# Eight small row sums split five and three around ScalarE's copies, in a fused RWKV-6 and mixture-of-depths kernel

## The chip, the core and the metric

The kernel runs on one core of a Trainium2 chip. The engines used are TensorE (PE in the profile, its weight loads PEld), VectorE (DVE), ScalarE (ACT), GpSimd (POOL) and SyncE (SP), which here only issues DMAs. Each engine works through its own instructions in the order in which the program gives them; semaphores make it wait for others. The metric is the device time of one execution in microseconds. Before the change, four runs took 201.69, 201.75, 202.72 and 203.75 us; their median is 202.24 us.

## What is computed

The first stage is an RWKV-6 recurrence over 768 steps for 4 batches and 8 heads of 48 channels. The second is a mixture of depths: each batch's 128 best rows of 768 get a small two-layer network.

```python
for t in range(S):                                   # per batch and head
    cur = (u * k[t])[:, None] * v[t][None, :]
    y[t] = r[t] @ (state + cur)
    state = w[t][:, None] * state + k[t][:, None] * v[t][None, :]
x = y as (B, S, H*D)
scores = x @ w_gate                                  # per batch
top = the 128 rows with the highest scores
out = x;  out[top] += sigmoid(scores[top]) * (relu(x[top] @ w1) @ w2)
```

The term with `u` is, for each row and head, one number times `v[t]`: the sum over the 48 channels of `r * k * u`. The kernel calls these eight numbers per row the row's *own* sums.

## The kernel before, in words

The sequence is cut into chunks of 128 rows, 6 per batch, 24 in all (`n` = 0 to 23). In a chunk the recurrence becomes matrix products: running products of the decays (two scans on VectorE, L285 and L296) scale r and k, then scores, a mask, and output = masked scores times v, plus r times the carried state. The function `turn(i)` (L704) does in one pass parts of several chunks: it finishes chunk i-1, does the main work of chunk i and prepares i+1 and i+2. It is called with i from -2 to 24. `tc.manual_schedule()` keeps the order that the code gives, engine by engine.

What a turn makes of the engines that the change touches, in ScalarE's order (i is the turn):

- `first_left` (L304), one column;
- `own_values(i)` (L360): for each of 8 heads an activation with `Copy` over 48 elements whose accumulator is the head's own sum; the profile shows each as an ACTIVATE and an ACTIVATION_READ_ACCUMULATOR at L364. Their input `rk` is made by GpSimd in L355 (r times k) and L358 (times u);
- `compared(i-2)`: TensorE spreads a chunk's scores as a transposed tile `ps_e` (L519, the one buffer `psW`), VectorE counts with it who is ahead of whom (L521, L525), and ScalarE copies it to `every` (L530). The copy waits for L525, and the next user of `psW`, the transposes `ps_w` of the decays (L265 through `decays_t`), waits for the copy;
- `back(i)`: the copy `kt` (L404), which `carry_products` (TensorE, `ps_kv`, L474) needs;
- `rows_out(i-1)`: the copy `x` (L443); GpSimd adds `vo` to it (L444), and L449 and L454 make the row scores. In the last two turns VectorE does this instead, with no ScalarE copy;
- `own_results(i)`: own sum times v. For chunks 1 to 8 GpSimd does four heads and ScalarE four (L377), for the others GpSimd does all eight (L373);
- `fed_in_turn`: a few products of the network of an earlier batch, and at its steps the ReLU copy `hid` (L634);
- `range_check(i+2)` (L332); `carry_products(i)`, whose result ScalarE copies to `kvs` (L480) for n below `AHEAD` (L89, here 9); `outputs_t(i)` with the copy `yt` (L432). `ps_yt` and the next turn's scores `ps_s` (L386) share the one buffer `psS`, so `ps_s` waits for this copy.

`carry(i-1)` (L487 and after) adds the chunk's product to the carried state: for n below `AHEAD` with GpSimd from `kvs`, for later chunks with VectorE from PSUM; GpSimd then multiplies by the decay (L494). VectorE's order in a turn is: this add, scaled `K` (L343), L521, L525, the mask `sc` (L394), scaled `R` (L343), scan L285, L291, L293, scan L296.

At the start, `u` and `w_gate`, one row each, are put in all 128 partitions by `spread` (L255): a product of a row of ones (one row by 128 columns) with the row (one by 384). `warm` (L249) runs products of a zero tile `nothing` before the data is there. `nc.any.memset` (L143) leaves the choice of the engine to the recording layer.

Of the kernel before, what the change touches and what calls it, by code (L numbers as in the profile page):

```python
# [10 lines left out]
FP32 = mybir.dt.float32  # L11
BF16 = mybir.dt.bfloat16
# [6 lines left out]
L = 128  # L19
# [5 lines left out]
def _rows(ap, n):  # L25

    return dataclasses.replace(ap, ap=[[0, n]] + [list(x) for x in ap.ap])
# [10 lines left out]
def kernel(  # L38
# [40 lines left out]
    nc = tc.nc  # L79
    PSUM = bass.MemoryType.PSUM  # L80

    B, H, S, D = r.shape
    C = H * D
# [2 lines left out]
    NCH = S // L  # L86
    HP = H // 2

    AHEAD = S // L + 3  # L89
    NDC = C // L  # L90
    NFC = F // L
    NHF = NCH // 2
# [7 lines left out]
    setup = ctx.enter_context(tc.tile_pool(name="setup", bufs=1))  # L100
    lev = ctx.enter_context(tc.tile_pool(name="lev", bufs=2))
# [26 lines left out]
    for queue, hs in ((nc.sync, slice(H // 2, H)), (nc.scalar, slice(0, H // 2))):  # L128
        queue.dma_start(
            out=w_bufs[0][:, hs, 0:D], in_=w[0, hs, 0:L, :].rearrange("h t d -> t h d")  # L130
        )

    u_row = setup.tile([1, C], FP32)
    nc.scalar.dma_start(out=u_row, in_=_rows(u.rearrange("h d -> (h d)"), 1))
    wg_row = setup.tile([1, C], FP32)
    nc.scalar.dma_start(out=wg_row, in_=_rows(moe_w_gate, 1))
    u_bc = consts.tile([L, H, D], FP32)
    wg_bc = consts.tile([L, C], FP32)
    nothing = setup.tile([L, 512], BF16)
    nc.vector.memset(nothing, 0.0)  # L140
    for i in range(NBUF):
        for bufs, value in ((w_bufs, 1.0), (k_bufs, 0.0), (r_bufs, 0.0), (v_bufs, 0.0)):
# [10 lines left out]
    def loads(n):  # L153
        load(v_bufs, v, n - 3)
        load(k_bufs, k, n - 1)
        load(r_bufs, r, n - 1)
        load(w_bufs, w, n)
# [19 lines left out]
    def load_weights(n):  # L177
        while n > 0 and weights:
            to, src = weights.pop(0)
            nc.sync.dma_start(out=to, in_=src)  # L180
            n -= 1


    ident = consts.tile([L, L], FP32)
    make_identity(nc, ident)
    minus = consts.tile([L, 1], BF16)
    nc.vector.memset(minus, -1.0)
    one_row = setup.tile([1, L], FP32)
    nc.vector.memset(one_row, 1.0)
    ones_f = consts.tile([L, 1], FP32)  # L190
    nc.vector.memset(ones_f, 1.0)
    high = consts.tile([L, 1], FP32)
# [20 lines left out]
    for t, sign in ((before_f, 1), (after_f, -1)):  # L213
        nc.gpsimd.memset(t, 1.0)
        nc.gpsimd.affine_select(
            out=t, in_=t, pattern=[[sign, L]], base=-1, channel_multiplier=-sign,
# [32 lines left out]
    def warm(n):  # L249

        ps = psM.tile([L, 512], FP32, tag="m", name="ps_n")
        for _ in range(n):
            nc.tensor.matmul(ps, nothing[:, 0:L], nothing, start=True, stop=True)

    def spread(to, row):  # L255

        ps = psM.tile([L, C], FP32, tag="m", name="ps_b")
        nc.tensor.matmul(ps, one_row, row, start=True, stop=True)
        nc.scalar.copy(out=to, in_=ps)
# [46 lines left out]
    def check_sums():  # L306

        above = setup.tile([L, 1], FP32)
        nc.vector.tensor_reduce(out=above, in_=guard, axis=AX.X, op=ALU.add)
        below = setup.tile([L, 1], FP32)  # L310
        junk = setup.tile([L, N * HP], FP32)
        nc.vector.tensor_scalar(
            out=junk, in0=alls.rearrange("p n j -> p (n j)"), scalar1=float(LOW ** L),
            scalar2=None, op0=ALU.is_lt, op1=ALU.add, accum_out=below,
        )
        return above, below
# [40 lines left out]
    def own_weights(t):  # L357
        nc.gpsimd.tensor_mul(t["rk"], t["rk"], u_bc)  # L358

    def own_values(t):  # L360
        rk = t.pop("rk")
        o = t["own"] = lev.tile([L, H], FP32, tag="own", name="own")
        for h in range(H):
            nc.scalar.activation(  # L364
                out=rk[:, h, :], in_=rk[:, h, :], func=AF.Copy, accum_out=o[:, h:h + 1]
            )

    def own_results(t):
        n, own = t["n"], t.pop("own")
        vo = t["vo"] = lev.tile([L, H, D], FP32, tag="vo", name="vo", bufs=3)  # L370
        vt = v_bufs[n % NBUF]
        some = H // 2 if 0 < n < AHEAD else H
        nc.gpsimd.tensor_mul(  # L373
# [93 lines left out]
    def carry_products(t):  # L467
# [4 lines left out]
        for j in range(HP):  # L472
            for q in (0, 1):
# [3 lines left out]
                )  # L477
        if n < AHEAD:
            t["kv"] = lev.tile([L, HP, D], FP32, tag="kvs", name="kvs")
            nc.scalar.copy(out=t["kv"], in_=kv)  # L480

    def carry(t, nxt):
# [6 lines left out]
        new = state[n + 1] = lev.tile([L, HP, D], FP32, tag="state", name="state")  # L489
        aside = n < AHEAD  # L490
        if n in state:
# [171 lines left out]
    def step(f, n, *more):  # L663
        if 0 <= n < N:
            f(work.setdefault(n, dict(n=n)), *more)

    def mix(n=1, place=None):


        while n > 0 and mixing:  # L670
            if place is not None and mixing[0][1] not in (None, place):
                return
            try:
                mixing[0][1] = next(mixing[0][0])
                n -= 1
            except StopIteration:
                mixing.pop(0)
# [16 lines left out]
    def fed_in_turn(n, few):  # L694

        kept = (feed or picked) and (feed or picked)[0][0] == B - 2
        fed(few if kept else n, on=False)
# [6 lines left out]
    def turn(i):  # L704
        soon = i >= N - 1
        step(first_left, i + 1)
        if i < 1:
            step(scaled_aside, i + 1, "K", "right")
        step(own_products, i + 1)
        step(scores, i)  # L710
        step(own_values, i)
        step(carry, i - 1, work.get(i))
        if i > 0:
            step(scaled, i + 1, "K", "right")
        if i >= 0:
            step(own_weights, i + 1)
        if soon:
            step(masked, i)
        if i == N - 1:
            sums.extend(check_sums())  # L720
        if i < N:
            step(compared, i - 2)
        step(back, i)
        mix(place="half")
        if not soon:
            step(masked, i)
        step(rows_out, i - 1, soon)
        step(row_scores_soon if soon else row_products, i - 1)
        step(own_results, i)
        fed_in_turn(PIECES // 2, 2 if i >= N - 1 else 1)  # L730
        step(inputs_t, i + 1, "R", r_bufs)
        if i == -1:
            spread(wg_bc, wg_row)
        step(scaled, i + 1, "R", "left")
        step(decays_t, i + 2)
        mix(place="mid")
        if i == -2:
            warm(2)
        step(range_check, i + 2)
        if i == -1:  # L740
            spread(u_bc.rearrange("p h d -> p (h d)"), u_row)
            step(own_weights, i + 1)
        step(carry_products, i)
        step(outputs_t, i)
        fed_in_turn(PIECES - PIECES // 2, 1 if i == N - 1 else 0)
        if i == N - 1:
            step(compared, i - 1)
        step(inputs_t, i + 2, "K", k_bufs)
        if i == -2:
            warm(1)  # L750
        if not soon:
            step(row_sums, i - 1)
        step(scans, i + 2)
        if 0 <= i - 2 < N - 1 and chunks[i - 2][1] == NCH - 1:
            mixing.append([mixture(chunks[i - 2][0]), "end"])
        mix(place="end")
        if i > -2:
            loads(i + 5)
        if i in WEIGHT_TURNS:
            load_weights(1)  # L760

    with tc.manual_schedule():
        warm(6)
        for i in range(-2, N + 1):
            turn(i)

        ended.append(True)
        mix(1000)
        mixing.append([mixture(B - 1), "half"])
        step(compared, N - 1)  # L770
        fed(1)
        mix()
        wide = checked(sums)
        fed(1)
        mix()
        fed(NFC - 2)
        mix(2)
        fed(2)
        mix(1000)
        fed(1000)  # L780
        outside = nc.values_load(wide, min_val=0, max_val=1)
# [72 lines left out]
```

## Time and profile before

| | |
|---|---|
| profiled execution | 201.88 us |
| span, first to last instruction | 200.2 us |
| median of the four runs | 202.24 us |
| TensorE busy, weight loads | 188.8 us (94%), 152.5 us (76%) |
| VectorE, GpSimd, ScalarE busy | 159.8, 138.6, 128.9 us |
| ScalarE, own sums (L364): 192 activations and 192 reads | 43.7 and 36.6 us busy, overlapping |
| ScalarE waiting for L525 before `every` (L530) | 12.0 us, 12 times |
| ScalarE waiting for `ps_yt` before `yt` (L432) | 27.2 us, 22 times |

Busy time of one engine can overlap itself, since an instruction's end and the next one's start are pipelined: eight own sums start 0.225 us apart although each ACTIVATE is listed with 0.23 us and each read with 0.19. Idle time on an engine matters only where the work that sets the end is waiting for it. The kernel has three stretches: up to about 12 us the first loads and the set-up; up to 68 us the first batch and a half, with several engines nearly full; from there to the end mostly TensorE, because the network of the earlier batches is fed between the chunks' products.

### The profile page before, as it was taken

How to read it: one execution, taken by the hardware profiler on the slowest of the kernel's cores; microseconds unless marked ns; L12 is line 12 of the kernel's file. 1: busy time of each engine (PE TensorE's matmuls, PEld its weight loads, DVE VectorE, ACT ScalarE, POOL GpSimd, SP SyncE). 2: the span in 40 equal slices, each digit the busy share in tenths (PEclk: the TensorE clock that was granted, in tenths of full speed). 3: DMA queues.
4: the chain of work that ended last, by engine and by line, in shares of the span. 5: the costliest groups of instructions: out<-in, count | busy, mean ns of one | idle time of the engine just before them, and what ended most of it. 6: DMA issues, size and time to landing. Idle time of an engine off the chain costs nothing.

```text
span 200.2 us, 6416 instructions
## 1 busy us (share of the span) xinstructions
PE 188.8 (94%) x2289; PEld 152.5 (76%) x2289; DVE 159.8 (80%) x347; ACT 128.9 (64%) x659; POOL 138.6 (69%) x183
## 2 busy tenths in 40 slices
PE   7989999999899999999999999999999998999980
PEld 3578787777777788897887888897887997866840
DVE  6999899999999978988979888989978983961010
ACT  4489899989976966787366776787366686410300
POOL 8498899896895996769539798768639796121201
PEclk9999999999999999999999999999999999999997
DMA  7999999999979999999983894996664131111101
GB/s 114 163 163 165 172 192 193 239 207 258 192 110 260 229 145 241 219 233 176 192 153 94 145 216 100 139 170 136 147 93 114 35 92 44 39 44 41 39 8 44
DMA packets 105387, 28.81 MB, mean 144 GB/s; under 512 B 100482, under 2 KB 104580, under 8 KB 105348
## 3 DMA queue, kind: packets, MB, share of 16 engines
q1 hardware_dynamic: 104304, 26.65, 74.1%
q0 software_dynamic: 512, 1.57, 2.5%
q8 instruction: 20, 0.33, 0.7%
q14 instruction: 19, 0.16, 0.3%
q10 hardware_dynamic: 532, 0.10, 0.3%
HBM read 22.81 MB, written 5.51 MB: 141 GB/s over the span
## 4 chain that ended last, share of the span: by engine, by line
PE 61%; DVE 5%; ACT 2%; POOL 2%; issue 1%; POOLq 0%; DVEq 0%
PE ps_h L629 11%; PE ps_f L641 11%; PE ps_s L386 8%; PE ps_yt L419 6%; PE ps_t L265 6%; PE ps_kv L474 4%; PE ps_yt L427 4%; PE ps_w L265 3%; PE ps_y L272 3%; PE ps_t L272 2%; PE ps_e L519 2%; DVE pick L562 1%; ACT rk L364 1%; PE ps_r L545 1%; PE ps_x L593 1%
## 5 line engine op out<-in xcount | busy, mean ns | idle before, releaser
L364 ACT ACTIVATE rk<-rk 128x48 f32<-128x48 f32 x192 | 43.7, 232 | 0.1
L364 ACT ACTIVATION_READ_ACCUMULATOR rk<-rk 128x1 f32 x192 | 36.6, 191 | 0.0
L444 POOL TENSOR_TENSOR x<-x,vo 128x384 f32<-128x384 f32 x22 | 22.2, 1007 | 19.7 <-ACT x L443 19.6
L432 ACT COPY yt<-ps_yt 128x512 f32<-128x512 f32 x24 | 14.1, 587 | 27.2 <-PE ps_yt L427 24.2
L394 DVE TENSOR_TENSOR sc<-ps_s,before_f 128x1024 f32<-128x1024 f32 x24 | 29.3, 1219 | 2.9 <-PE ps_s L386 2.9
L296 DVE TENSOR_TENSOR_SCAN left<-ps_w,from_left 128x511 f32<-128x511 f32 x24 | 30.7, 1280 | 0.9
L285 DVE TENSOR_TENSOR_SCAN right_buf<-ps_w,from_right 128x511 f32<-128x511 f32 x24 | 29.1, 1212 | 1.0 <-PE ps_w L265 0.8
L386 PE MATMUL ps_s<-R,K 48*128 48x128 f32 x384 | 27.9, 285 | 1.8 <-ACT yt L432 0.9
L386 PEld LDWEIGHTS ps_s<-R,K 48*128 48x128 f32 x384 | 23.3, 187 | 6.0 <-ACT yt L432 3.6
L629 PE MATMUL ps_h<-xeT,w 128*128 128x128 f32 x192 | 25.6, 280 | 0.2 <-ACT hid L634 0.2
L419 PE MATMUL ps_yt<-sc,v_buf 128*64 128x128 f32 x384 | 25.6, 275 | 0.0
L358 POOL TENSOR_TENSOR rk<-rk,u_bc 128x384 f32<-128x384 f32 x24 | 24.1, 1005 | 1.2 <-DVE alls L291 0.8
L629 PEld LDWEIGHTS ps_h<-xeT,w 128*128 128x128 f32 x192 | 22.9, 192 | 2.3 <-issue 1.3
L355 POOL TENSOR_TENSOR rk<-r_buf,k_buf 128x384 f32<-128x384 f32 x24 | 24.1, 1004 | 0.0
L641 PE MATMUL ps_f<-w,hid 128*128 128x384 f32 x64 | 23.8, 500 | 0.0
L449 POOL TENSOR_TENSOR scr<-x,wg_bc 128x384 f32<-128x384 f32 x22 | 22.0, 1000 | 1.7
L419 PEld LDWEIGHTS ps_yt<-sc,v_buf 128*64 128x64 f32 x384 | 20.6, 137 | 0.8 <-issue 0.5
L343 DVE TENSOR_TENSOR R<-ps_t,left 128x512 f32<-128x512 f32 x24 | 16.5, 686 | 3.7 <-ACT own L607 1.3
L373 POOL TENSOR_TENSOR vo<-v_buf,own 128x384 f32<-128x384 f32 (+1 forms) x24 | 17.3, 722 | 1.4 <-ACT rk L364 1.4
L343 DVE TENSOR_TENSOR K<-ps_t,right_buf 128x512 f32<-128x512 f32 x22 | 15.0, 680 | 3.4 <-PE ps_t L265 3.4
L265 PE MATMUL ps_w<-ident,w_buf 128*128 128x128 f32 x96 | 15.5, 285 | 0.6 <-ACT every L530 0.3
L641 PEld LDWEIGHTS ps_f<-w,hid 128*128 128x128 f32 x64 | 11.0, 190 | 6.0 <-issue 1.1
(115 smaller groups left out, 361.9 us busy)
## 6 DMA issues: line engine op xcount, KB each, us to landing
k_buf<-in_k_dram SPq DMA_DIRECT2D x24, 192.0 KB, 5.2
r_buf<-in_r_dram SPq DMA_DIRECT2D x24, 192.0 KB, 5.2
v_buf<-in_v_dram SPq DMA_DIRECT2D x24, 192.0 KB, 4.0
out_dram<-x SPq DMA_DIRECT2D x24, 192.0 KB, 2.4
w_buf<-in_w_dram SPq DMA_DIRECT2D x23, 192.0 KB, 4.7
w<-in_moe_w_dram SPq DMA_DIRECT2D x3, 512.0 KB, 6.0
w<-in_moe_w_dram SPq DMA_DIRECT2D x4, 384.0 KB, 5.9
w_buf<-in_w_dram ACTq DMA_DIRECT2D x1, 96.0 KB, 3.3
```

What stands on the lines that cost most here:

```text
L265: nc.tensor.transpose(ps[:, j, :], src(j), ident)
L285: nc.vector.tensor_tensor_scan(out=flat[:, W - 2::-1], data0=wt[:, W - 1:0:-1], data1=from_right.rearrange("p j t -> p (j t)")[:, W - 2::- ...
L296: nc.vector.tensor_tensor_scan(out=left.rearrange("p j t -> p (j t)")[:, 1:W], data0=wt[:, 0:W - 1], data1=start.rearrange("p j t -> p (j ...
L343: nc.vector.tensor_mul(out, t.pop(name + "t"), t.pop(by))
L355: nc.gpsimd.tensor_mul(rk, r_bufs[n % NBUF][:, :, 0:D], k_bufs[n % NBUF][:, :, 0:D])
L358: nc.gpsimd.tensor_mul(t["rk"], t["rk"], u_bc)
L364: nc.scalar.activation(out=rk[:, h, :], in_=rk[:, h, :], func=AF.Copy, accum_out=o[:, h:h + 1])
L386: nc.tensor.matmul(ps[:, q, j, :], t["K"][rows, j, :], t["R"][rows, j, :], start=True, stop=True,)
L394: nc.vector.tensor_mul(t["sc"].rearrange("p q j t -> p (q j) t"), ps.rearrange("p q j t -> p (q j) t"), _heads(before_f, 2 * HP),)
L419: nc.tensor.matmul(ps[half(c), j % 2, j // 2, :], vt[:, 2 * j + q, :], t["sc"][:, q, j, :], start=(j < 2), stop=(old is None), skip_group_ ...
L629: nc.tensor.matmul(ps[:, q, :], w1[:, dc, (f0 + q) * L:(f0 + q + 1) * L], xeT[:, dc, :], start=(dc == 0), stop=(dc == NDC - 1),)
L641: nc.tensor.matmul(ps, hid[:, fc, :], w2[:, fc, :], start=(fc == 0), stop=(fc == NFC - 1))
```

## The change

Three edits:

1. `own_values` is called twice in a turn. The first five heads stay where all eight were, the last three come after `rows_out` and the row products, just ahead of `own_results`.
2. `AHEAD` falls from 9 to 8. For chunk 8 alone, the copy `kvs` and the four activations of L377 go from ScalarE, VectorE adds the carry from PSUM, and GpSimd multiplies all eight heads of `vo`.
3. `one_row`, `u_row` and `wg_row` get 128 rows, zero but for the first, so that the products of `spread` run over 128 rows. GpSimd sets them ahead of the other set-up, and ScalarE's two small loads wait for that. `nothing` becomes one column, which the warming products read as broadcast. As a result the recording layer also puts the set-up fills of L143 on other engines: ScalarE has three in place of four; VectorE takes two that were ScalarE's and gives it one, and has a shorter fill of `nothing` and none of `one_row`.

The order of TensorE's products and of SyncE's DMAs is unchanged.

```diff
-    AHEAD = S // L + 3
+    AHEAD = S // L + 2
+
+    FIRST = H * 5 // 8
...
-    u_row = setup.tile([1, C], FP32)
-    nc.scalar.dma_start(out=u_row, in_=_rows(u.rearrange("h d -> (h d)"), 1))
-    wg_row = setup.tile([1, C], FP32)
-    nc.scalar.dma_start(out=wg_row, in_=_rows(moe_w_gate, 1))
+    one_row = setup.tile([L, L], FP32)
+    u_row = setup.tile([L, C], FP32)
+    wg_row = setup.tile([L, C], FP32)
+    for t, src in ((u_row, u.rearrange("h d -> (h d)")), (wg_row, moe_w_gate)):
+        nc.gpsimd.memset(t, 0.0)
+        nc.scalar.dma_start(out=t[0:1, :], in_=_rows(src, 1))
...
-    nothing = setup.tile([L, 512], BF16)
+    nothing = setup.tile([L, 1], BF16)
...
+    nc.gpsimd.memset(one_row, 0.0)
+    nc.gpsimd.memset(one_row[0:1, :], 1.0)
...
-    one_row = setup.tile([1, L], FP32)
-    nc.vector.memset(one_row, 1.0)
...
-            nc.tensor.matmul(ps, nothing[:, 0:L], nothing, start=True, stop=True)
+            nc.tensor.matmul(
+                ps, nothing.to_broadcast([L, L]), nothing.to_broadcast([L, 512]),
+                start=True, stop=True,
+            )
...
-    def own_values(t):
-        rk = t.pop("rk")
-        o = t["own"] = lev.tile([L, H], FP32, tag="own", name="own")
-        for h in range(H):
+    def own_values(t, heads):
+        rk = t["rk"]
+        if heads[0] == 0:
+            t["own"] = lev.tile([L, H], FP32, tag="own", name="own")
+        o = t["own"]
+        for h in heads:
...
-        step(own_values, i)
+        step(own_values, i, range(FIRST))
         step(carry, i - 1, work.get(i))
...
         step(row_scores_soon if soon else row_products, i - 1)
+        step(own_values, i, range(FIRST, H))
         step(own_results, i)
```

## The prediction

> **What bounds the kernel now.** I read the chain of work that ended last first. From 68.17 us to 167.7 it is TensorE without a gap; before that it passes through VectorE, GpSimd and ScalarE. So the front (to 68 us), the middle and the tail are costed apart. The groups of instructions give ScalarE's sums:
>
> ```profile
> L364 ACT ACTIVATE rk<-rk 128x48 f32<-128x48 f32 x192 | 43.7, 232 | 0.1
> ```
>
> In the timeline eight take 1.82 us (22.25 to 24.07), 0.225 each pipelined; three are 0.67 us. Busy time by stage (columns: stage, length, busy of PE, PEld, DVE, ACT, POOL, then clock and DMA):
>
> ```profile
> 22.00:28.00 6.00, 5.88 (x87) 4.82 (x87) 5.45 (x10) 5.61 (x31) 5.06 (x8) 1.00 0.98 189
> ...
> 34.00:40.00 6.00, 5.88 (x87) 4.83 (x87) 5.83 (x12) 5.61 (x31) 5.47 (x8) 1.00 1.04 230
> ```
>
> A front turn lasts 6 us, and nobody has much to spare. Its loop, in the timelines of ScalarE and TensorE (start, duration):
>
> ```profile
> 35.83 0.23 ACT L364 ACTIVATE rk<-rk 128x48 f32<-128x48 f32 x1
> ...
> 36.05 0.25 ACT L530 COPY every<-ps_e 128x128 f32<-128x128 f32 x1
> ...
> 39.16 0.59 ACT L432 COPY yt<-ps_yt 128x512 f32<-128x512 f32 x1 [0.39 <-PE ps_yt L427]
> ```
>
> ```profile
> 35.82 0.60 PE L265 MATMUL ps_t<-ident,r_buf 128*128 128x128 f32 x4
> 36.36 0.66 PE L265 MATMUL ps_w<-ident,w_buf 128*128 128x128 f32 x4
> ...
> 38.43 0.65 PE L427 MATMUL ps_yt<-R,state 64*48 64x128 f32 x16
> 39.02 0.66 PE L265 MATMUL ps_t<-ident,k_buf 128*128 128x128 f32 x4
> 39.79 1.16 PE L386 MATMUL ps_s<-R,K 48*128 48x128 f32 x16
> ```
>
> `ps_w` starts when `every` (behind eight sums) ends; ps_yt, `yt`, `ps_s` follow. TensorE stalls twice: before `ps_w` 36.36 - 36.26 = 0.10 (four transposes issue in 0.44) and before `ps_s` 0.33, behind the `yt` copy.
>
> **Edit 1, front.** VectorE's mask `sc` (L394) is the ruler. It starts at 11.85, 17.27, 23.54, 29.54, 35.53 and 41.52 in turns 0 to 5; intervals 5.42, 6.27, 6.00, 5.99, 5.99. In the last VectorE has no idle time: 0.55 for L521, 0.27 for L525, so 5.17 for the rest. With L521 at 0, 0.27, 0.40 (its issue spacing or duration), VectorE's floors are 5.17, 5.44, 5.71, 5.84, 5.99. Excess 0.25 + 0.83 + 0.29 + 0.15 + 0 = 1.52 us: more the front can't give.
>
> What the path gives:
> - Turn 0. The timeline has
>
> ```profile
> 13.28 0.45 ACT L404 COPY kt<-ps_t 128x384 f32<-128x384 f32 x1
> ...
> 13.78 0.67 PE L474 MATMUL ps_kv<-v_buf,kt 128*64 128x48 f32 x16 [0.94 <-ACT kt L404]
> ```
>
> `kt` waits only for the sums, which start at 11.45: five end at 12.57, `kt` 0.67 earlier, `ps_kv` at about 13.05 (v landed at 12.51). ScalarE then has three sums, L332 and `kvs` before `yt`: 14.55, and `ps_yt` ends at 14.6. So `yt` and `ps_s(1)` come 0.7 earlier. `sc(1)` can use 0.19 of it: VectorE's K ends at 17.08.
> - Turn 1. No `every` yet; TensorE's 0.7 lead runs through `ps_kv(1)` (18.1 for 18.96) to `ps_s(2)` at 20.9 for 21.81, `ps_e` at 22.0, L525 at 22.35, `sc(2)` at 22.63: 5.55 in place of 6.27, gain 0.72. The loads keep ahead (w of chunk 3 landed at 16.14, v1 17.33, k3 18.55).
> - Turns 2 and 3. Without the 0.10 stall TensorE's cycle is 5.88, as the `yt` stall stays: 0.12 and 0.11.
> - From turn 4 VectorE has no gap to 61.6 us; the gain is carried, not added to.
>
> Sum 0.19 + 0.72 + 0.12 + 0.11 = 1.14 us; bounds 0 and 1.52. GpSimd's x (L444) is released 0.67 earlier and its own sums for `vo` 0.67 later, but with L444 and L449 (2.0 us) between.
>
> **Junction, 61 to 68 us, with edit 2.** The chain of waits passes from the index (L575) to GpSimd's gather, x, the row products, then ScalarE L454, the sums, `every`, `ps_w` at 68.17. All shift by the front's 1.14. ScalarE loses three sums before `every` (0.67), but L525 ended at 67.46 and edit 2 puts VectorE's add (0.27) ahead of it; `every` at 67.46 + 0.27 + 0.06 = 67.79 for 67.87: 0.08. What edit 2 takes off ScalarE (four L377, 0.92; `kvs`, 0.21) ends before an idle gap: the `yt` of turn 8 waits 0.39 for TensorE. GpSimd trades 0.59 (L493) for 0.32 more of L373: nothing. Bounds: 0.29 (TensorE's stall at `ps_w`) gained, 0.27 (the add) lost. I take 0.1.
>
> **Middle.** TensorE is continuous, so only lateness could cost. Three sums behind `every` are 0.67 us later work, and `yt` afterwards waited 1.02 to 2.61 us in every turn from 9 to 22. `hid` at 90.12 and 134.68 is needed by L641 at 92.44 and 137.0. Gain: at 83.10 and 127.67 `ps_w` takes 0.60 instead of 0.44 behind a late `every`; five sums remove that: 2 x 0.16 = 0.32, at worst 0.
>
> **Tail.** In the last chunk's turn the sums after `every` land ahead of `hid`; no L404 or L443 stands between:
>
> ```profile
> 171.87 0.27 ACT L530 COPY every<-ps_e 128x128 f32<-128x128 f32 x1 [1.26 <-DVE ahead L525]
> 172.03 0.60 ACT L634 ACTIVATE hid<-ps_h 128x512 f32<-128x512 f32 x1
> 172.58 0.59 ACT L432 COPY yt<-ps_yt 128x512 f32<-128x512 f32 x1
> ```
>
> All eight sums fitted in front of the 1.26 us wait. Now three follow it, `hid` starts at 172.70, and TensorE's L629 (172.69, already 0.18 late for `hid`) moves by 0.67. The `ps_y` behind it needs `yt`, also 0.67 later; then the last scores, ranks and gather in series. A loss of 0.67; queued behind the sums are `hid`, `yt` and the last copies of `every`.
>
> **Edit 3.** GpSimd gets two fills of 384 columns (about 0.41 each, between 0.20 for 128 and 0.52 for 512) and two small ones, some 1.0 us. It is idle for 2.35 us before 7.43, and `ident` would be ready near 2.3, needed at 3.84. ScalarE's row loads issue at 1.34 and 2.04, the fills end near 1.25 and 1.65: no wait; if 0.3, it is before a 2.3 us idle. The first transposes wait for w (3.74 and 4.10). A load of 1 row by 128 takes 182 ns, of 128 by 128 190; L258's two halves issue 0.43 apart at 1 row, L641's 0.33 at 128: between 0 and a 0.2 gain, taken 0. The zero fill falls from 0.27 to about 0.06, so warming starts 0.21 sooner. A broadcast moving operand isn't in the trace; the broadcast weights of L519 load in 133 ns against 143. Bounds: 0, or twice the 0.427 spacing: six products end at 1.06 + 5.12 = 6.18, 2.3 us late. The nearest row says 0.
>
> Matmuls are slow until 6.46 us (transposes 0.213 apart) and then fast (0.109) at a granted clock of 1.00 throughout. The Trainium skill ("TensorE: Matmul & The Clock Gate", section "What's actually happening") says a free-running window of 3.4 us releases the clock; by it a 0.21 us earlier start has about 0.21 / 3.4 = 6% to gain a window (estimate from that page), and the sum would be some 0.4 us less. No row here shows it.
>
> **Sum.** -1.14 - 0.1 - 0.32 + 0.67 = -0.89 us. The profiled execution: 201.88 to 201.0. It lies 0.36 under the median of the runs; from that, 202.24 to 201.35.
>
> The skill speaks against a gain: "Perfetto Trace Analysis", section "Identifying the Most-Contended Engine", says to optimize the engine with the highest occupancy. That is TensorE (94%; weight loads 76%), whose work isn't changed; by it only the tail's loss remains, 202.9. The stage rows say that the front is shared.
>
> **Rivals.**
> 1. VectorE holds the front already; only turn 0's 0.19 comes. -0.19 - 0.32 + 0.67 = +0.16: 202.4. For it: no idle time from turn 4. Against it: 0.45 us idle before L525 at 23.26.
> 2. Slower: ScalarE behind `every` becomes the loop. From L525: 0.38 to `every`, 2.65 + 0.67 to `yt`, 0.63 to `ps_s`, 1.10 to `ps_e`, 0.36 to L525: 5.79 us. It decides above TensorE's 5.88. If the 0.39 us before `yt` is all that can absorb 0.67, turns 2 to 7 lose 0.28 each, 1.7, for 1.14 gained: +0.56 - 0.32 + 0.67 = +0.9: 203.15.
> 3. The tail's 0.67 is hidden: 200.7.
> 4. The start: the clock is released a window later, or the broadcast is slow: slow and fast spacing differ by 0.104 per transpose and about 0.2 per 512 columns; 16 transposes and two spreads make 1.7, the broadcast 2.3. With the rest about 203.3.
>
> **Chances.** Forecast 0.5; rivals 1: 0.16, 2: 0.13, 3: 0.12, 4: 0.09. The range goes from rival 3 less a part of the 1.52 - 1.14 left (200.4) to rival 2 (203.1). A measurement of this kernel tells about 1% from no change, the four runs being 1% apart: 200.2 and 204.3 are the bounds. Faster by over 1% needs rival 3 with the larger bounds: 0.08; slower needs rival 4 on top of a loss of rival 2: 0.07.
>
> **What would show it.** `kt` of turn 0 near 12.6, `sc` of turns 1, 2 and 5 near 17.1, 22.6 and 40.4; `ps_w` that opened the middle near 66.9; the `ps_w` of the two turns without `kt` at 0.44; `hid` three sums behind `every` in the tail. Wrong, if `yt` no longer waits for TensorE in turns 2 to 7, or if the clock is released at another time.

## The result, and the profile after

The changed kernel takes 201.54 us in the median; the kernel before, measured beside it, takes 201.86. The medians differ by 0.32 us. The ratio is one of means, 0.9967 with a 95% interval of [0.9954, 0.9979]: 0.7 us less, a change of a third of a per cent. (Every ratio here leaves out executions over 1.5% above the same kernel's fastest: one of the kernel before, 216.03 us, and below two of e1_split, 204.04 and 204.31.) The profiled execution took 201.40 us against 201.88, its span 199.7 us against 200.2. The forecast was 201.35 us, "same" the likeliest. The total lies near it, but not because every term held: the front gave less than forecast, the start, costed at nothing, gave part of it back, and the four runs from whose median the forecast started lay 0.38 us too high (point 7 below).

The mask `sc` on VectorE is the ruler again. The table takes the start of the mask in some turns, and of `hid` in the last chunk's turn (172.03 us before), and subtracts the start in the kernel before (profiled executions, us; negative is earlier).

| where | after | forecast | what lies between it and the row above |
|---|---|---|---|
| mask of turn 0 | -0.42 | 0 | the set-up (edit 3) |
| mask of turn 1 | -0.70 | -0.19 | turn 0 |
| mask of turn 2 | -0.38 | -0.91 | turn 1 |
| mask of turn 5 | -0.70 | -1.14 | turns 2 to 4 |
| mask of turn 10 | -0.80 | -1.24 | junction, edit 2 |
| mask of turn 23 | -1.12 | -1.56 | middle |
| `hid` in the last chunk's turn | -0.43 | -0.89 | tail |

The two masks of turn 2, from VectorE's timelines before and after, show how the table is read:

```profile
23.54 1.22 DVE L394 TENSOR_TENSOR sc<-ps_s,before_f 128x1024 f32<-128x1024 f32 x1
```

```profile
23.16 1.22 DVE L403 TENSOR_TENSOR sc<-ps_s,before_f 128x1024 f32<-128x1024 f32 x1
```

So junction (0.10), middle (0.32) and tail (0.69 lost) came as forecast within 0.02 us. The front gave 0.28 us from the mask of turn 0 to that of turn 5, instead of 1.14, and the set-up gave 0.42 that was costed at nothing.

The groups of the changed kernel (columns as before: busy us, mean ns, then the idle time ahead). The own sums cost what they did; `every` now waits longer for VectorE, because it stands behind five sums:

```profile
L373 ACT ACTIVATE rk<-rk 128x48 f32<-128x48 f32 x192 | 44.3, 238 | 0.2 <-POOL rk L365 0.2
L539 ACT COPY every<-ps_e 128x128 f32<-128x128 f32 x20 | 5.3, 264 | 21.6 <-DVE ahead L534 21.6
```

The same two stretches of the front by stage (columns as before). ScalarE is busy 5.83 of 6 us in both, where it had 5.61. A turn's work is what it was; up to turn 4 the turn lasts 5.84 us now, so a slice of 6 us can hold more than one:

```profile
22.00:28.00 6.00, 5.88 (x93) 5.00 (x91) 5.12 (x10) 5.83 (x33) 5.46 (x8) 1.00 1.02 188
34.00:40.00 6.00, 5.88 (x91) 4.92 (x87) 5.89 (x12) 5.83 (x34) 5.61 (x8) 1.00 1.12 219
```

ScalarE's timeline of the changed kernel (start, duration): first turn 0, then one turn of the front, then the last chunk's turn.

```profile
12.21 0.46 ACT L413 COPY kt<-ps_t 128x384 f32<-128x384 f32 x1
...
34.96 0.27 ACT L539 COPY every<-ps_e 128x128 f32<-128x128 f32 x1 [0.17 <-DVE ahead L534]
...
38.31 0.58 ACT L441 COPY yt<-ps_yt 128x512 f32<-128x512 f32 x1
...
170.75 0.27 ACT L539 COPY every<-ps_e 128x128 f32<-128x128 f32 x1 [1.94 <-DVE ahead L534]
170.92 0.25 ACT L373 ACTIVATE rk<-rk 128x48 f32<-128x48 f32 x1
...
171.60 0.58 ACT L643 ACTIVATE hid<-ps_h 128x512 f32<-128x512 f32 x1
172.08 0.58 ACT L441 COPY yt<-ps_yt 128x512 f32<-128x512 f32 x1
```

`kt` of turn 0 starts 1.07 us earlier than before: 0.67 for the three sums that were ahead of it, 0.40 for the earlier start. `yt` at 38.31 no longer waits for TensorE. In the tail the three sums stand between `every` (170.75) and `hid` (171.60), 0.68 us of sums, where `hid` followed `every` directly before.

TensorE's timeline of the changed kernel in the front. The stall at `ps_w` is gone (35.57 follows the four transposes at their 0.44), the one at `ps_s` is still 0.33:

```profile
35.13 0.60 PE L272 MATMUL ps_t<-ident,r_buf 128*128 128x128 f32 x4
35.57 0.60 PE L272 MATMUL ps_w<-ident,w_buf 128*128 128x128 f32 x4
...
38.18 0.66 PE L272 MATMUL ps_t<-ident,k_buf 128*128 128x128 f32 x4
38.95 1.16 PE L395 MATMUL ps_s<-R,K 48*128 48x128 f32 x16
```

And in turns 0 and 1; the front's gain was lost in turn 1:

```profile
12.72 0.67 PE L483 MATMUL ps_kv<-v_buf,kt 128*64 128x48 f32 x16 [0.41 <-ACT kt L413]
...
18.58 0.67 PE L483 MATMUL ps_kv<-v_buf,kt 128*64 128x48 f32 x16 [0.61 <-DMA v_buf<-in_v_dram]
```

`ps_kv` of turn 0 is 1.06 us earlier. `ps_kv` of turn 1 waits 0.61 us for chunk 1's v, which had landed at 17.33 in the kernel before. The chain of waits (start, duration, what) runs through that load:

```profile
12.05 6.40 DMA v_buf<-in_v_dram
18.45 0.14 issue
18.58 0.67 PE ps_kv L483 x16
```

The trace has 16 landings for this load of 192 KB, as many as there are DMA engines. 15 of them were there at 17.22, the last at 18.45. Ahead of that the DMA engines carried something else besides the loads, as the DMA view of the stretch 14 to 17 us shows (queue, kind: packets, MB, share of 16 engines' time):

```profile
q8 instruction: 1, 0.02, 3.0%
```

That is one packet of 16 KB of program code (3.0% of 16 times 3 us is 1.44 us), and its record starts at 14.60. In the kernel before the same fetch started at 18.34, when v was there. That the fetch holds back the last part is inferred from the two times; the view doesn't say which engine carried it.

TensorE's clock differs as well. A trace's first clock record begins where the clock is first granted in full: at 6.79 us before, at 3.92 in the changed kernel. (Ahead of its first record a view shows 1.00, which the forecast read as a clock of 1.00 throughout.) TensorE's first transposes, before and after, agree with it (four of them issue 0.21 to 0.24 apart before, 0.11 to 0.16 after):

```profile
3.88 1.08 PE L265 MATMUL ps_w<-ident,w_buf 128*128 128x128 f32 x4
```

```profile
3.86 0.68 PE L272 MATMUL ps_w<-ident,w_buf 128*128 128x128 f32 x4
```

### The profile page after: what moved, and what is told of

Read it like the earlier page. It is cut to its first block, busy times and chain, and to the rows that moved or that the text cites. A ratio compares the mean times of both kernels' runs of the same rounds, so it can differ in the third digit from the quotient of the medians.

```text
span 199.7 us, 6426 instructions
## 1 busy us (share of the span) xinstructions
PE 186.5 (93%) x2289; PEld 151.7 (76%) x2289; DVE 159.7 (80%) x348; ACT 127.5 (64%) x653; POOL 139.1 (70%) x186
## 4 chain that ended last, share of the span: by engine, by line
PE 71%; ACT 9%; DMA 6%; SPq 5%; DVE 4%; issue 2%; POOL 0%; POOLq 0%; DVEq 0%
PE ps_h L638 11%; PE ps_s L395 11%; PE ps_f L650 11%; PE ps_yt L428 7%; PE ps_t L272 6%; SPq L152 5%; PE ps_kv L483 4%; PE ps_yt L436 4%; PE ps_y L279 4%; PE ps_w L272 4%; DMA v_buf<-in_v_dram 3%; PE ps_t L279 3%; PE ps_e L528 3%; DMA r_buf<-in_r_dram 3%; ACT yt L441 2%; ACT vo L386 2%
## 5 line engine op out<-in xcount | busy, mean ns | idle before, releaser
L373 ACT ACTIVATE rk<-rk 128x48 f32<-128x48 f32 x192 | 44.3, 238 | 0.2 <-POOL rk L365 0.2
L373 ACT ACTIVATION_READ_ACCUMULATOR rk<-rk 128x1 f32 x192 | 37.3, 194 | 0.0
L539 ACT COPY every<-ps_e 128x128 f32<-128x128 f32 x20 | 5.3, 264 | 21.6 <-DVE ahead L534 21.6
```

The costliest lines, as they stand in the source:

```text
L373: nc.scalar.activation(out=rk[:, h, :], in_=rk[:, h, :], func=AF.Copy, accum_out=o[:, h:h + 1])
```

## The experiments

Twelve kernels ran, in three sets of four. Each row of the table gives the times beside the kernel before of the same set. The last five columns are the profiled execution's gain over the kernel before by stretch: to the mask of turn 0 (start), from mask 0 to 5 (front), 5 to 10 (junction), 10 to 23 (middle), and from there to `hid` (tail).

| kernel | median us | ratio, interval | start | front | junction | middle | tail |
|---|---|---|---|---|---|---|---|
| e1_split | 201.66 | 0.9949 [0.9916, 0.9982] | 0.12 | 0.99 | 0.16 | 0.33 | -0.69 |
| e2_ahead | 201.79 | 0.9986 [0.9956, 1.0015] | 0.13 | -0.01 | -1.04 | 0 | 0 |
| e3_rows | 201.60 | 0.9960 [0.9927, 0.9994] | 0.22 | 0.15 | -0.01 | 0.01 | 0 |
| e4_tail | 200.37 | 0.9889 [0.9847, 0.9931] | 0.28 | 1.13 | -0.94 | 0.33 | 0 |
| e5_fill | 200.12 | 0.9899 [0.9875, 0.9923] | 0.51 | 0.13 | 0.09 | 0.34 | 0 |
| e6_fill_before | 201.75 | 0.9994 [0.9976, 1.0013] | 0.10 | -0.03 | -0.02 | -0.02 | 0 |
| e7_nine | 200.26 | 0.9907 [0.9880, 0.9934] | 0.40 | 0.84 | 0.08 | 0.32 | 0 |
| e8_column | 201.58 | 0.9985 [0.9957, 1.0013] | 0.31 | 0.01 | 0.03 | 0.01 | 0 |
| e9_v0 | 200.24 | 0.9930 [0.9911, 0.9950] | 0.27 | 0.89 | 0.09 | 0.33 | 0 |
| e10_four | 200.66 | 0.9947 [0.9929, 0.9965] | 0.36 | 0.77 | -0.13 | 0.33 | 0 |
| e11_six | 200.53 | 0.9945 [0.9928, 0.9962] | 0.35 | 0.64 | 0.14 | 0.33 | 0 |
| e12_twice | 203.28 | 1.0090 [1.0065, 1.0115] | 0.17 | 0 | -0.48 | -0.01 | 0 |

(The medians of the kernel before in the three sets, e1 to e4, e5 to e8 and e9 to e12, were 202.23, 201.75 and 201.61 us, so medians of different sets are not compared without it. Why they differ is told under the clock, below.)

### One edit at a time, and the tail repaired

**e1_split** is edit 1 alone:

```diff
+    FIRST = H * 5 // 8
...
+        step(own_values, i, range(FIRST))
...
+        step(own_values, i, range(FIRST, H))
```

> Edit 1 alone, on the kernel before. Theory A (the terms of the prediction add): the front gains 0.3 to 1.1 us, the two turns without kt 0.16 each, the tail loses 0.66; net -0.8 to 0 us, so a ratio of 0.996 to 1.000, and in the trace the last chunk's hid starts about 0.7 us after every, with ps_w at 0.44 in the two turns without kt. Rival B (the whole gain is in the start, edit 3): the split is worth nothing, ratio 1.000 +- 0.001 or above.

**e2_ahead** is edit 2 alone:

```diff
-    AHEAD = S // L + 3
+    AHEAD = S // L + 2
```

> Edit 2 alone, on the kernel before. Both theories: almost nothing. VectorE's add (0.27 us) goes in front of the mask of turn 9, but there ScalarE's sums end last (every at 67.87 for an earliest 67.79). Between -0.1 and +0.3 us, ratio 0.9995 to 1.0015.

**e3_rows** is edit 3 alone (the diff of the set-up and of `warm` shown with the change):

```diff
+    one_row = setup.tile([L, L], FP32)
+    u_row = setup.tile([L, C], FP32)
+    wg_row = setup.tile([L, C], FP32)
...
+    nothing = setup.tile([L, 1], BF16)
```

> Edit 3 alone, on the kernel before: zero column for warming, rows spread by products of 128 rows. Theory A: the first matmuls run at the slow spacing or not by the place of the clock's release; where it comes before the first transposes, the first mask is 0.3 us earlier, and VectorE carries that to the end: about -0.2 to -0.3 us at the median, 0.9985 to 0.999. Rival B: it removes the runs of the kernel before that take 202.7 and 203.8 us, and the gain in the mean is 0.3% or more, ratio 0.997 or less, with the fastest runs unchanged near 201.6.

**e4_tail** is the full change, but with all eight sums in front in the last chunk's turn:

```diff
-        step(own_values, i, range(FIRST))
+        step(own_values, i, range(FIRST if i < N - 1 else H))
...
-        step(own_values, i, range(FIRST, H))
+        if i < N - 1:
+            step(own_values, i, range(FIRST, H))
```

> The changed kernel, but in the last chunk's turn all eight sums stand in front again. Theory A: the tail's loss of 0.66 us goes, hid starts 0.16 us after every there, and all else stays; 200.8 to 200.9 us, ratio to before 0.9935 to 0.9945. Rival B: nothing else can move, as the sums are off the path; 201.5, ratio 0.997.

Measured. The profile of edit 1 alone is close to the forecast's front. `kt` of turn 0 starts at 12.49 (forecast near 12.6), v of chunk 1 landed at 17.14, `ps_kv` of turn 1 goes without a wait, and the mask of turn 5 stands at 40.41 (forecast 40.4; 0.12 of the gain is from the start). TensorE's timeline of e1_split:

```profile
12.99 0.67 PE L478 MATMUL ps_kv<-v_buf,kt 128*64 128x48 f32 x16 [0.26 <-ACT kt L408]
18.17 0.67 PE L478 MATMUL ps_kv<-v_buf,kt 128*64 128x48 f32 x16
```

Its gains are 0.99, 0.16 and 0.33, its loss in the tail 0.69; forecast for edit 1 were 1.14, about 0.1, 0.32 and 0.67. Its ratio of 0.9949 is below the expected 0.996; over all its twelve executions the ratio of the means is 0.9972. Edits 2 and 3 are small: edit 2 moved no mask of turns 1 to 8 against that of turn 0 by more than 0.02 us, and edit 3 was 0.22 us ahead at the mask of turn 0 and 0.36 from turn 1 on, which was carried to the end. The ratio of e3_rows, 0.9960, is as low as its rival B asked for; among the executions that kept the clock its median is 0.26 us under that of the kernel before, which is theory A's size.

e4_tail has the same program as the changed kernel up to the last chunk's turn, so its profile is also a second one of that front: 1.13 us, with v of chunk 1 landed at 17.27. In the tail nothing was lost; ScalarE's timeline of e4_tail:

```profile
171.08 0.27 ACT L539 COPY every<-ps_e 128x128 f32<-128x128 f32 x1 [1.26 <-DVE ahead L534]
171.24 0.60 ACT L643 ACTIVATE hid<-ps_h 128x512 f32<-128x512 f32 x1
```

The wait of `every` is 1.26 us again, as in the kernel before: the eight sums fit in front of it. This version beats both kernels.

So the terms add roughly, as theory A had it: the mask of turn 5 is 1.11 us earlier with edit 1, 0.37 with edit 3, and 1.41 (e4_tail) and 1.24 (e7_nine, below) with both. The gain of edit 1 is there without any of edit 3, which rules out rival B, by which the start would hold the whole gain.

What remained open was the loss of 0.94 and 1.04 us in the junction of e2_ahead and e4_tail, all of it between the masks of turns 8 and 9. TensorE's timeline of e4_tail there:

```profile
58.75 0.83 PE L578 MATMUL ps_i<-ids,pick 128*128 128x2 bf16 x5 [0.42 <-DVE pick L571]
59.44 0.73 PE L279 MATMUL ps_y<-turned,yt 112*128 112x112 f32 x4
60.00 1.11 PE L272 MATMUL ps_t<-ident,r_buf 128*128 128x128 f32 x4
60.91 1.06 PE L272 MATMUL ps_w<-ident,w_buf 128*128 128x128 f32 x4
```

Four transposes take 1.06 to 1.11 us where they take 0.60 to 0.66 elsewhere. Busy time by stage of e4_tail (the figure after the bracket of POOL is the granted clock) says why:

```profile
56.32:59.73 3.41, 2.99 (x41) 2.42 (x39) 3.27 (x10) 1.56 (x13) 2.24 (x4) 1.00 0.81 131
59.73:63.14 3.41, 3.41 (x32) 2.92 (x31) 3.41 (x7) 2.30 (x11) 2.39 (x3) 0.50 0.99 293
```

TensorE's clock was halved for 3.41 us; in e2_ahead the same from 60.67 to 64.08. Just ahead of it TensorE waits for `pick` (0.42 us here, 0.27 there, 0.28 in the kernel before, 0.43 in the changed one) amid six products of two columns. How busy TensorE is there doesn't tell: in the window of 3.41 us ahead of the fall it was busy 2.99 us in e4_tail, and in the window that holds this wait also 2.99 in the changed kernel, whose clock held. The clock of every execution is on record, and it sorts them: of 63 executions of the kernel before in the three sets, the 42 with a mean clock of at least 0.990 took 201.38 to 202.23 us, the 21 with less (0.983 or lower) took 202.37 or more, in groups near 202.7 and 203.7. They were 14 of 29, 6 of 23 and 1 of 11 in the three sets, which is why the medians of the sets differ. (The mean has a second part: in every profile the clock falls to 0.50 again for the last 0.6 to 4.1 us, so that a mean of 0.990 or 0.989 by itself doesn't show a loss.) The next four kernels test whether the wait at `pick` is the cause.

### The wait ahead of the index product, the two small edits

**e5_fill** is e4_tail with two warming products ahead of the first batch's `ps_i`:

```diff
+            if b == 0 and not ended:
+                warm(2)
             ps = psK.tile([L, 2], FP32, tag="kv", name="ps_i")
```

> The changed kernel with all eight sums in front in the last chunk's turn (as in the run before it), and two products of the zero column (128 x 512) ahead of the index product ps_i of the first batch, where TensorE otherwise waits 0.28 to 0.43 us for pick. Theory C (TensorE's clock): in some executions the thin work and the wait around ps_i (58 to 60 us) let the granted clock fall to 0.50 for 3.4 us, which costs about 1.05 us at 62 us. Then the two products take the slow executions away: runs close together near 199.9 to 200.1, median some 0.4 us under the 200.37 without them, mean granted clock about .996, and in the profile no step between turns 8 and 9. Rival D (the step is chance of another kind, a late load or a code fetch): median 200.4 as without, or 0.1 to 0.2 more for the added products, and the spread of 1.1 us stays.

**e6_fill_before** is the kernel before with the same two lines.

> The kernel before, with the same two products ahead of the first batch's ps_i and nothing else. Theory C: the kernel before has the same low stretch (its runs lie in clusters near 201.8, 202.7 and 203.8); with the products the two upper clusters go, runs near 201.7, median 0.2 to 0.4 us under that of the kernel before. Rival D: runs as before, in the same clusters.

**e7_nine** is e5_fill without edit 2:

```diff
-    AHEAD = S // L + 2
+    AHEAD = S // L + 3
```

> As e5_fill, but AHEAD is 9 again (edit 2 undone). From the profiles of edit 1 alone (0.15 us gained between the masks of turns 9 and 10) and of the full change (0.09 us gained over turns 8 to 10), theory A: edit 2 is worth nothing beside edit 1, or costs 0.06; median within 0.1 us of e5_fill. Rival: edit 2 carries part of the junction's gain; then this kernel is 0.2 us or more slower than e5_fill.

**e8_column** is the kernel before with the warming operand of edit 3 alone:

```diff
-    nothing = setup.tile([L, 512], BF16)
+    nothing = setup.tile([L, 1], BF16)
...
-            nc.tensor.matmul(ps, nothing[:, 0:L], nothing, start=True, stop=True)
+            nc.tensor.matmul(
+                ps, nothing.to_broadcast([L, L]), nothing.to_broadcast([L, 512]),
```

> The kernel before with the warming operand as one column read as broadcast, and nothing else of edit 3. If the gain of 0.22 to 0.38 us that edit 3 shows at the masks of turns 0 and 1 comes from TensorE's earlier start (the zero fill takes 0.06 in place of 0.27), it is here too: masks 0.2 to 0.4 earlier, first products about 0.2 earlier, and the spacing of transposes falls before 6.4 us. If it comes from the products over 128 rows or from the moved fills, the masks of turns 0 and 1 are as before, within 0.05.

Measured. e5_fill: 199.93 to 200.23 us, and one execution of 200.89, the profiled one. Its clock held; it had lost 0.5 us in turn 1, to the same wait as the changed kernel, 0.86 us for v. The median was 0.25 us under e4_tail's, not 0.4, and that is a difference of sets: beside its own kernel before, e4_tail has 0.9889 and e5_fill 0.9899, which the intervals don't tell apart. TensorE's timeline of e5_fill at the place shows no wait any more:

```profile
59.16 0.38 PE L257 MATMUL ps_n<-nothing 128*128 128x512 bf16 x1
59.38 0.97 PE L580 MATMUL ps_i<-ids,pick 128*128 128x2 bf16 x6
```

e6_fill_before missed theory C's numbers: its median is that of the kernel before, since that one's median lay in the lower group in this set (6 of 23 executions under a clock of 0.990). Two of 12 executions still lost their clock, 202.51 and 202.68 us. By itself this decides nothing.

e7_nine is 0.14 us slower than e5_fill, within what the intervals tell apart: edit 2 is worth nothing beside edit 1, as theory A had it. Its add is seen at the mask of turn 9, which in the changed kernel and in e5_fill is 0.27 us later than its neighbours, and is made good by turn 10.

e8_column has the start's gain: 0.31 us at the mask of turn 0, 0.35 at the end. The kernels without any of edit 3 lie between 0 and 0.17 there, those with its warming operand between 0.22 and 0.51. So most of edit 3's gain comes from this operand; TensorE's first product starts at 1.01 us instead of 1.27. As a time the gain is not settled, since the interval of e8_column includes 1.

### The load, the number of sums, a longer wait

**e9_v0** is e5_fill, but chunk 1's carry product reads chunk 0's v:

```diff
-                    v_bufs[n % NBUF][:, 2 * j + q, 0:D], start=True, stop=True,
+                    v_bufs[0 if n == 1 else n % NBUF][:, 2 * j + q, 0:D], start=True, stop=True,
```

> As e5_fill, but the carry product of chunk 1 (ps_kv) reads chunk 0's v in place of chunk 1's, so the state carried on from there is another one; the work is the same. Theory E: what the changed kernel lost in turn 1 (0.5 us at the mask of turn 2) is ps_kv's wait for v1, whose last part is held back to 18.45 to 18.52 us when a 16 KB code fetch starts as early as 14.6 to 14.8 us. Without that wait only ps_yt behind it can still wait, for about 0.2. Then the slowest executions of e5_fill (200.9) move down: runs between 199.8 and 200.5, median 199.9 to 200.1, and the mask of turn 2 is at 32.9 to 33.2 in the profile whenever the fetch runs. Rival: the lost 0.5 us has another cause in turn 1 (VectorE or ScalarE late); then a mask of turn 2 near 33.6 and times near 200.9 still occur.

**e10_four** and **e11_six** are e5_fill with another split:

```diff
-    FIRST = H * 5 // 8
+    FIRST = H * 4 // 8
```

> As e5_fill with FIRST = 4: four sums ahead of ScalarE's copies, four behind (all eight ahead in the last chunk's turn). By rival 2's loop, which the profile of the changed kernel shows at 5.84 us a turn (from every to ps_s and back) with three sums behind, a fourth makes it 6.07, above TensorE's 5.88 and VectorE's 5.99: turns 2 to 7 lose 0.08 to 0.19 each, 0.5 to 0.6 in all; median 200.6 to 200.8, masks of turns 3 to 7 6.05 to 6.08 apart. If ScalarE's loop has more slack than that, it is as e5_fill, 200.1, or 0.1 faster.

> As e5_fill with FIRST = 6: six ahead, two behind. By the prediction's terms kt of turn 0 comes 0.45 earlier than in the kernel before in place of 0.67, so up to 0.22 of turn 1's 0.72 is lost; the stall at ps_w is gone as with five; the loop is 5.61 and never binds. 0.1 to 0.2 slower than e5_fill: 200.2 to 200.35. If the gain of the front hangs on the number behind every (rival 2 active in turns 2 to 5), it is 0.1 to 0.2 faster than e5_fill: 199.9 to 200.0.

**e12_twice** is the kernel before with more for VectorE to do ahead of `ps_i`:

```diff
-            for c in range(NCH):
+            for c in ([0, 1, 2] if b == 0 else []) + list(range(NCH)):
```

> The kernel before, in which VectorE writes the first three pick tiles of the first batch twice (0.3 us each), so that TensorE's wait ahead of ps_i grows from 0.28 to about 1.2 us. Theory C (the granted clock falls to 0.50 for 3.4 us when a window of low work ends near this wait; 21 of 52 executions of the kernel before have a mean clock under 0.990): with a longer wait nearly all executions lose the clock, each at 1.05 us or more on top of the 0.9 us that VectorE's work itself may cost: median 203.2 to 204, mean clocks at most .990, the profile with 0.50 somewhere between 59 and 66 us. Rival D (the clock's drop has nothing to do with this wait): only the 0.9 us, median 202.6 or less, and the same share of low clocks as before.

Measured. (The expectation of e9_v0 gives the mask of turn 2 on a scale of its own: its 33.6 is the mask that the changed kernel has at 23.16 on the page, so its 32.9 to 33.2 are some 22.4 to 22.8. That of e12_twice has a miscount: it was 20 of 52.)

e9_v0: in the profile the fetch started early again, at 14.35, and the last part of v landed at 18.21; `ps_kv` started at 18.13 without waiting, the mask of turn 2 stood at 22.71, and the front gave 0.89 us. With the wait it had given 0.28 (the changed kernel) and 0.13 (e5_fill). So the wait for v is what those two lost. The times don't follow: they went from 200.00 to 200.84 us, with every clock at 0.990 or above, so theory E's narrower spread did not come. Something else spreads these executions, and it is open.

e10_four has a median 0.42 us above that of e9_v0 in its own set and 0.54 above that of e5_fill in the set before; the loop's price was 0.5 to 0.6. ScalarE's timeline of e10_four:

```profile
34.51 0.27 ACT L539 COPY every<-ps_e 128x128 f32<-128x128 f32 x1 [0.39 <-DVE ahead L534]
...
40.51 0.27 ACT L539 COPY every<-ps_e 128x128 f32<-128x128 f32 x1 [0.39 <-DVE ahead L534]
```

A turn takes 6.00 us, and `every` waits 0.39 for L534 in each turn, which waits for the scores, which wait for `yt`: rival 2's loop, closed. The forecast's own sum for it (5.79 with three sums behind, so 6.02 with four) is nearer than the 6.05 to 6.08 of the expectation. In the changed kernel the same loop closes in 5.84 us from turn 2 to turn 4 (`every` at 23.28, 29.12, 34.96).

e11_six has a median 0.29 us above that of e9_v0 and 0.41 above that of e5_fill. In the profile it loses what was expected: `kt` of turn 0 starts at 12.62, where e7_nine, with five sums ahead and no wait for v either, has 12.36, and the mask of turn 2 stands at 22.88 for 22.63, which is one sum. ScalarE's timeline of e11_six shows something about turns 2 and 3 as well:

```profile
28.84 0.27 ACT L539 COPY every<-ps_e 128x128 f32<-128x128 f32 x1
...
32.19 0.58 ACT L441 COPY yt<-ps_yt 128x512 f32<-128x512 f32 x1 [0.18 <-PE ps_yt L436]
...
34.68 0.27 ACT L539 COPY every<-ps_e 128x128 f32<-128x128 f32 x1
```

With only two sums behind `every` the turn is 5.84 us too, and `yt` waits for TensorE again. So TensorE's own cycle is 5.84 there, not the forecast's 5.88; with three sums behind, the loop and TensorE bind at the same length.

e12_twice: TensorE's wait ahead of `ps_i` grew to 0.76 us, and five of six executions lost their clock (means 0.978 to 0.985, 203.08 to 204.46 us), against 1 of 11 of the kernel before in the same set. The sixth kept it (0.991) and took 202.09; it is the profiled one, and shows 0.48 us more in the junction, VectorE's own added work. Theory C's 203.2 to 204 holds for the median, rival D's equal share does not. The profiled one also shows that a longer wait does not always bring the loss.

In the other direction: with edit 1 and the two filling products 0 of 30 executions had a mean clock under 0.990 (e5_fill, e7_nine, e9_v0, e10_four, e11_six); with edit 1 and without them it was 14 of 72 (the changed kernel, e1_split, e4_tail), four of them at 0.989. The 14 come from other sets than the 30, and the kernel before lost its clock less often in the sets of the 30 (7 of 34) than in that of e1_split and e4_tail (14 of 29), so part of this difference may be the set's. That a longer wait at `pick` makes the loss more frequent is shown, by e12_twice within one set; that filling the wait prevents it fits, but is not shown, since e6_fill_before still lost the clock in 2 of 12.

## Why the prediction was right, point by point

1. **Turn 0 and turn 1 (0.19 + 0.72).** The mechanism is right and shown: 0.99 us of front in e1_split and 1.13 in e4_tail, for 1.14 forecast (0.84 in e7_nine, which starts 0.40 us earlier; its mask of turn 2 stands at the forecast 22.63). In the changed kernel's own profile it failed, at the sentence "The loads keep ahead (... v1 17.33 ...)". That landing was read from one execution as if it were fixed. Of the 14 profiles, the three in which the 16 KB fetch started at 14.35 to 14.77 us (the changed kernel, e5_fill, e9_v0) have the last part of v at 18.21 to 18.52; the other eleven, with the fetch at 15.6 us or later, have it at 17.1 to 17.4. (In six of these the fetch began at 15.6 to 16.2, before v had landed, and v was not late, so the coincidence is close but the mechanism is not shown.) With `ps_kv` at 18.96, as before, such a delay was harmless; moved to 18.0 by the change, it costs 0.5 us. The gain of 0.9 us was put right up to a transfer whose landing has a spread of 1.4 (17.14 to 18.52). What sets the time of the fetch isn't settled: the same program up to the tail fetched at 14.60 and at 17.29.
2. **Turns 2 and 3 (0.12 + 0.11).** Measured 0.16 and 0.15 in the changed kernel. What the forecast had named as a sign of being wrong, a `yt` that no longer waits for TensorE, did appear: rival 2's loop closes in 5.84 us here. But e11_six keeps 5.84 with a loop that is one sum shorter, so TensorE's cycle is 5.84 as well, and the forecast's 5.88 was 0.04 too long. That the two bounds meet is why the number held.
3. **VectorE's floor.** From turn 5 the gain was only carried, in every profile.
4. **Junction (0.1) and middle (2 x 0.16).** 0.10 and 0.32 in the changed kernel. The middle's 0.31 to 0.34 is there in every version that has edit 1, in two steps at the two turns without `kt`.
5. **Tail (0.67 lost).** 0.69 lost, and 0 with the eight sums back in front. This was the dearest avoidable step of the change.
6. **Edit 3 (0).** Mis-sized: 0.42 us at the mask of turn 0 in the changed kernel; from kernel to kernel 0.22 to 0.51 with the warming operand and 0 to 0.17 without, so about a quarter of a microsecond. The text had "warming starts 0.21 sooner" and allowed it only a small chance to matter. The other sign of being wrong, a clock released at another time, appeared too, at 3.92 us instead of 6.79. But e7_nine, e9_v0 and e11_six, released at 6.87 to 6.91 as late as the kernel before, have 0.27 to 0.40 us at the mask of turn 0, so the gain doesn't need the earlier release. The broadcast operand cost nothing, so rival 4 is out.
7. **The sum.** By the profiled executions -0.48 instead of -0.89: 0.86 less in the front, 0.42 more at the start, the rest alike. By the ratio -0.67. That figure has a part which no term of the forecast holds: the changed kernel's executions lost their clock more rarely, 9 of 54 by a mean clock under 0.990 (three of them at 0.989), against 28 of 78 of the kernel before, whose clocks are not on record here and which are counted above 202.3 us, the limit that the clocks gave in the three sets. Among those that kept it the medians are 201.50 and 201.75, only 0.25 apart. Why the change lowers that share is not shown. And the forecast took its 0.89 off 202.24, the median of four runs, two of which took 202.72 and 203.75; the 78 executions have 201.86. From there the sum gives 200.97, and the measured 201.54 is 0.57 above it. So the median of 201.54 lies near the forecast 201.35 by luck: the sum was too hopeful by 0.2 us (by the ratio), 0.4 (by the profiles) or 0.6 (by the medians), and its start 0.38 too high.

Rivals: 1 (VectorE holds the front) falls with 0.99 and 1.13 us of front. 2 has a real mechanism at the wrong price: with three sums behind the loop is no longer than TensorE's cycle; one more sum makes it the bound. 3 falls by the tail's 0.69. The page of the Trainium skill that the forecast held against a gain ("Perfetto Trace Analysis", section "Identifying the Most-Contended Engine") asks to judge TensorE's headroom by its arithmetic or its weight loads; the loads' 76% lie below VectorE's 80%, so the forecast's reading that it names TensorE is not secure. The gain came from the order of work on ScalarE, busy 64%.

The version with the lowest median is edit 1, all eight sums in front in the last chunk's turn, and two products ahead of the first `ps_i`: e5_fill at 200.12 us, 0.9899 [0.9875, 0.9923] of the kernel before, an interval that lies below the changed kernel's [0.9954, 0.9979] as well. From e4_tail and e7_nine it is not told apart, so neither the two products nor edit 2 makes a difference to the time that was measured.

## What to carry to other kernels

When a change moves work earlier, list the loads that it moves up to and give each the spread of its landing over several profiles, not its one time. Splitting a block of small operations around the copies that others wait for pays up to the point where the loop through the later half reaches the next bound, here five of eight; the loop can be summed beforehand from the rows of one turn (6.02 us summed with four sums behind, 6.00 measured). And a split that pays in the steady turns should be looked at again in the last one, where everything behind it runs in series.

## What the runs showed of the hardware

- TensorE's granted clock fell to 0.50 for 3.41 us in two profiles (e2_ahead, e4_tail) in which TensorE had waited for only 0.27 and 0.42 us, between small products. In the 14 profiles the stretches at full clock last 194.56, 191.15, 187.73, 133.12 or 54.61 us, which are 57, 56, 55, 39 and 16 times 3.413. Each of these two losses cost 1.0 to 1.1 us, and it depends on the execution whether one comes.
- The Trainium skill ("TensorE: Matmul & The Clock Gate", section "What's actually happening") gives a free-running window of 3413 ns, and these stretches agree with it. The same page (section "HAM oscillation — how this bites in real kernels") puts the idle time that throttles at over about 3.4 us; the records here differ: the clock fell where TensorE had waited about a tenth as long. What sets it off is not shown.
- The clock's first release came between 3.92 and 6.91 us in the 14 profiles, for one and the same order of first products. The mask of turn 0 moves by 0.17 us between the five kernels that have the set-up of before, and by 0.29 between the eight that have all of edit 3.
- The first fetch of 16 KB of program code was one packet of 1.45 us in each of the 14 profiles. In the three in which it began by 14.77 us, the last part of a load of 192 KB landed 1.0 to 1.5 us after the other fifteen, and in the two whose next product needed it TensorE waited for it (0.61 and 0.86 us).
